# A first Fourier stage issued in half steps: four PSUM banks at once become two and two, three half units apart

## The chip, the cores and the metric

The kernel runs on one core of a Trainium2 chip. The metric is the device time of one execution in microseconds; the kernel before takes 2130.23 us (median of three runs, 2129.25 to 2134.58).

## What is computed

The reference chains three parts. The first transforms `x` (8 batches of 3072 rows and 256 columns, float32) along the rows, mixes its columns, and transforms it back:

```
X = np.fft.rfft(x, axis=1)
Xr, Xi = (X.real.astype(np.float32), X.imag.astype(np.float32))
Yr = Xr @ w_r - Xi @ w_i + b_r
Yi = Xr @ w_i + Xi @ w_r + b_i
Yr = np.sign(Yr) * np.maximum(np.abs(Yr) - lam, 0.0)      # Yi the same
y = np.fft.irfft(Y, n=x.shape[1], axis=1)
```

The second is a two-layer perceptron on all 24576 rows (256 to 2048 to 256, the hidden layer being a squared relu), and the third a soft mixture of 8 experts with 4 slots each. The change is in the first part alone.

## The kernel before

The transform of 3072 points is done as 48 times 64. **Stage A** is the transform of 48 points, **stage B** that of 64, then come the mixing of the columns (**L** and **S**) and the way back (**C**, and D in the next part). Intermediate results go through DRAM: `ad` after stage A, `zd` after stage C. TensorE does all products; VectorE (DVE), ScalarE (ACT) and GpSimd (POOL) take results out of PSUM, split them into a high and a low part and apply the threshold; nearly all transfers of this part are issued on SP's queue, in program order.

A **step** j of stage A (32 of them, four to a batch) takes two tiles `xt` of the input. `a_mm(j, q)` for q = 0 and 1 makes four products of 48 rows by 64 columns, one in each quadrant of the array, into two PSUM banks `psA`; each product is two instructions, so a step is two times eight. `a_out(j, q, r, copy)` copies one bank into half of the tile `sa` of r; with q = 1 the tile is complete, and its two writes to `ad` are issued. There are two buffers of the tag `sa`, so the first copy of a step for r waits until the write of the step before for the same r has landed. `load_x` fetches the tiles of the step after next; there are four `xt` buffers, so it must wait until `a_mm` has used the old ones.

Five steps are done ahead of the loop. The rest, 27, are woven into a loop over **half units** h from 0 to 203 (two to each of 96 units U), whose order is written out by hand and kept on every engine. In an even half TensorE gets `b_mm(U)` (psB), `l_mm(U-2)` (psL and psS) and then `first_stage`; in an odd half `c_mm(U-4)` (psC, only when U is odd) and then, at its end, `first_stage`. The consumers follow one half or one unit later: `b_hi` and `b_sum` on ACT, `b_lo`, `l_move` (L309, L310) and `l_soft` (L320) on DVE, the low part `Sl` on POOL, `c_out` on ACT. All products of this part share one pool of eight PSUM banks (`pbank`, tag `g`): a product waits until the former holder of its bank has been read.

`starts(j)` places the 27 steps at h = 0, 5, 10, 16, 22, 28 and so on, six halves apart. In its half a step is issued whole, followed by its four loads of `xt`; in each of the next four halves ACT copies one bank out. The writes to `ad` therefore come three and four halves after the step.

At the end of each half from h = 17 on, a generator `decode` is advanced, which fetches the perceptron's weights in 32 pieces (`raw`, two buffers) and works on them on all engines. It asks for piece n+1 when it begins with piece n, so the transfer stands in SP's queue behind all that was issued earlier, the step's loads of `xt` included. DVE's first instruction on a piece (L382) waits for its landing and holds up all that DVE has behind it.

Of the kernel before, what the change touches and what calls it, by code (L numbers as in the profile page):

```python
# [103 lines left out]
def fft_moe_kernel(ctx, tc, x, w_r, w_i, b_r, b_i, moe_w_in, moe_w_out, moe2_phi, moe2_w1, moe2_w2,  # L104
                   c_f1, c_bm, c_cm, c_dm, c_st, out):
    nc = tc.nc
    NB = x.shape[0]
# [17 lines left out]
    def drain(it):  # L125
        for _ in it:
            pass
# [26 lines left out]
    def weight_tiles():  # L154
        for q in range(NW):
            wia.append(wpool.tile([128, 4, 2, 128], F32R, tag=f"wia{q}", name=f"wia{q}"))
            wib.append(wpool.tile([128, 3, 2, 128], F32R, tag=f"wib{q}", name=f"wib{q}"))

    def early(tag, name):

        if tag.startswith("wia"):
            t = f(wpool.tile([128, 4, 2, 128], F32R, tag=tag, name=name).rearrange("p a b n -> p (a b n)"))
        else:
            t = wg[:, int(tag[2:])]
        return t.rearrange("p (a d) -> p a d", d=DM)
# [18 lines left out]
    NA = N2 // 16  # L184
# [3 lines left out]
    def pbank(name):  # L188
        return psP.tile([128, 512], F32, tag="g", name=name)

    def load_x(c):
        if c >= XL or c in xt:
            return
        b, k = divmod(c, NC)
        if c < NC:
            t = early(f"wia{c}", f"xt{c}")
        else:
            t = wka.tile([128, TX, DM], F32, tag="xt", name=f"xt{c}", bufs=XB)
        xv = x[b].rearrange("(n1 n2) d -> n1 n2 d", n2=N2)
        m = TX // 2 if c == 0 else TX  # L200
        for o in range(0, TX, m):
            for r in range(2):
                n = 16 * (k // 2) + 8 * r + 4 * (k % 2) + o
                nc.sync.dma_start(t[64 * r:64 * r + N1, o:o + m], xv[:, n:n + m])
        xt[c] = t

    def a_mm(j, q):
        b = j // NA
        if b not in ad:
            ad[b] = dram.tile([N1, N2, DM], F32, tag="ad", name=f"ad{b}", bufs=3)  # L210
        ps = [pbank(f"psA{j}_{q}_{r}").rearrange("p (a d) -> p a d", a=2) for r in range(2)]
        for r in range(2):
            for c in range(2):
                nc.tensor.matmul(ps[r][64 * c:64 * c + 64], lhsT=f1t[64 * r:64 * r + N1],  # L214
                                 rhs=xt[2 * j + c][64 * r:64 * r + N1, 2 * q:2 * q + 2], start=True, stop=True)
        for r in range(2):
            pa[j, q, r] = ps[r]
        if q:
            xt.pop(2 * j)
            xt.pop(2 * j + 1)  # L220

    def a_out(j, q, r, copy):
        i = 2 * j + r
        b, k = divmod(i, 2 * NA)
        if q == 0:
            sa[i] = early(f"wo{k}", f"sa{i}") if b == 0 else wka.tile([128, TX, DM], F32, tag="sa", name=f"sa{i}")
        copy(sa[i][:, 2 * q:2 * q + 2], pa.pop((j, q, r)))
        if q:
            t = sa.pop(i)
            for c in range(2):  # L230
                n = 8 * k + 4 * c
                (nc.sync if b else nc.scalar).dma_start(out=ad[b][:, n:n + TX], in_=t[64 * c:64 * c + N1])

    def load_b(u):
        b, k = divmod(u, NU)
        t = wkb.tile([128, 4, DM], F32, tag="bt", name=f"bt{u}")
        for ch in range(2):
            r = NP * ch + 2 * k
            nc.sync.dma_start(t[N2 * ch:N2 * ch + N2], ad[b][r:r + 4].rearrange("q n d -> n q d"))
        bt[u], bt[u + 1] = t[:, :2], t[:, 2:]  # L240
# [36 lines left out]
    def b_sum(u, eng):  # L277
        sf = sp[u].pop()
        h = wkb.tile([128, 2, 128], F32R, tag="Sh", name=f"Sh{u}")
        l = wkb.tile([128, 2, 128], F32R, tag="Sl", name=f"Sl{u}")  # L280
        split(h, l, sf, eng)
        sp[u] += [h, l]
# [206 lines left out]
    with tc.manual_schedule():  # L489
# [20 lines left out]
        EX = 1 if NB > 1 else 0  # L510
# [10 lines left out]
        def copy(j):  # L521
            return nc.scalar.copy if j % 2 else nc.vector.tensor_copy

        done = []
# [30 lines left out]
        nc.vector.tensor_copy(bias[1], bias[0])  # L555
        nc.vector.tensor_copy(bias[1][0:1, 1], bias[0][0:1, 0])
        dec_run = decode()
        aj = NA + EX
        if NB > 1:
            load_x(12)  # L560
            load_x(13)
# [5 lines left out]
        def at(u, *steps):  # L567
            if 0 <= u < NT:
                for g in steps:
                    g(u)  # L570

        def starts(j):
            j -= NA + EX
            return 5 * j if j < 3 else 16 + 6 * (j - 3)

        for h in range(2 * NT + 12):
            U, o = divmod(h, 2)

            def first_stage():
                nonlocal aj  # L580
                if aj < NB * NA and h == starts(aj):
                    for q in range(2):
                        a_mm(aj, q)
                        done.extend((aj, q, r) for r in range(2))
                    load_x(2 * aj + 4)
                    load_x(2 * aj + 5)
                    aj += 1
                elif done:
                    a_out(*done.pop(0), nc.scalar.copy)

            if o == 0:
                at(U, b_mm)
                at(U - 2, l_mm)
                at(U - 4, l_soft)
                at(U - 1, b_lo)
                at(U - 5, c_out)
                first_stage()
                at(U - 3, l_relu)
            else:
                at(U - 4, c_mm)  # L600
                at(U - 2, l_move)
                at(U, b_hi)
                at(U - 1, lambda u: b_sum(u, nc.gpsimd))
                first_stage()
                if U % 2 and U + 3 < NT:
                    load_b(U + 3)

            if h % 4 == 2 and h < 18:
                nc.sync.dma_start(bm[:, h + 6:h + 10], c_bm[:, h + 6:h + 10])
            if h % 4 == 1 and h < 24:  # L610
                nc.sync.dma_start(cm[:, h // 2:h // 2 + 2], c_cm[:, h // 2:h // 2 + 2])
            if h == 8:
                next(dec_run)
            if h == 14:
                nc.sync.dma_start(ident, c_st[:, 0])
                nc.sync.dma_start(dmt, c_dm)
                nc.sync.dma_start(phi, moe2_phi.rearrange("(a p) n -> p a n", p=128))
                nc.vector.memset(ss, 0.0)
                nc.vector.memset(nm[0], 3.0e38)
            if h == 16:  # L620
                weight_tiles()
            if h > 16:
                for _ in range(1 + (h % 4 == 0)):
                    next(dec_run, None)
            if U == NT - YL and o == 1:
                drain(dec_run)
                wkax.close()
                zp = wgt.enter_context(tc.tile_pool(name="zp", bufs=1, reuse_waits="tile"))
                yp[0] = ypx.enter_context(tc.tile_pool(name="yp0", bufs=1, reuse_waits="tile"))
                ylead = stage_d(0, pbank, nc.vector)  # L630
            if ylead is not None and U > NT - YL + 1:
                next(ylead, None)
# [258 lines left out]
        for n in range(NM + 2):  # L891
            sb, r = divmod(n, NW)
# [331 lines left out]
```

## Time and profile before

| | us |
|---|---|
| median of three runs | 2130.23 |
| profiled execution, device time | 2138.45 |
| its span, first to last instruction | 2136.7 |
| loop of half units within it | about 41.5 to 530 |
| stage A's last product | about 443 |

The profiled execution is 8.2 us longer than the median of the others. A row of the timeline gives start and duration in us, engine, line, operation, output and inputs, and the number of instructions merged; in brackets the idle time of the engine just before, and what ended it. PE is TensorE's product, PEld its weight load, SPq the queue of SP. The ends of products are modelled, so the time that a group of products takes is read from its first start to the start of the next group.

### The profile page before, as it was taken

What the parts mean: (1) busy time and instruction counts of PE and PEld (TensorE: products, weight loads), DVE (VectorE), ACT (ScalarE), POOL (GpSimd) and SP (SyncE); (2) the same over time, 40 slices, a digit from 0 to 9 for tenths busy, and PEclk for the clock granted to TensorE, in tenths of its full rate; (3) what the DMA queues carried; (4) which work ended last, traced back from release to release, by engine and by line L of the source; (5) the groups of instructions that cost most, each with busy time, mean ns of one, the idle gap of its engine ahead of it and who ended that gap; (6) DMA issues with size and microseconds to landing.
All of it is one profiled execution on the core that took longest, in us unless ns stands there. A gap on an engine that the chain in (4) does not pass through costs nothing.

```text
span 2136.7 us, 55389 instructions
## 1 busy us (share of the span) xinstructions
PE 2067.8 (97%) x22288; PEld 1617.6 (76%) x22288; DVE 1530.6 (72%) x2591; ACT 1272.8 (60%) x2910; POOL 1327.5 (62%) x1583
## 2 busy tenths in 40 slices
PE   7999999999799999999999999999999999999994
PEld 3788788888677777777777777777777777777743
DVE  2666776778377777777777777777777777777743
ACT  2577667765466665666665666666566666556632
POOL 0234333421577788887778888778888777888500
PEclk7999999999899999999999999999999999999995
DMA  8999898863211111111111121111111111111589
GB/s 237 250 233 240 221 240 235 246 174 95 46 27 28 29 35 29 33 37 28 28 35 29 29 43 27 28 28 37 29 30 40 27 28 33 32 29 47 172 311 400
DMA packets 113484, 209.75 MB, mean 98 GB/s; under 512 B 14060, under 2 KB 80620, under 8 KB 106956
## 3 DMA queue, kind: packets, MB, share of 16 engines
q1 hardware_dynamic: 112060, 203.04, 35.3%
q8 instruction: 175, 2.87, 0.6%
q10 hardware_dynamic: 1168, 3.18, 0.4%
q14 instruction: 81, 0.66, 0.1%
HBM read 122.38 MB, written 83.79 MB: 96 GB/s over the span
## 4 chain that ended last, share of the span: by engine, by line
PE 88%; DMA 5%; ACT 2%; DVE 1%; POOL 1%; issue 1%; SPq 1%; ACTq 0%; DVEq 0%; POOLq 0%
PE psX L701 20%; PE psA L701 19%; PE ls L754 9%; PE psZ L701 6%; PE pz_a L765 5%; PE psB L247 4%; PE psC L331 4%; PE psY L459 3%; PE pz L765 3%; PE psA L214 3%; PE pz_x L765 2%; PE psL L117 2%; PE psL L118 2%; PE psL L119 2%; DMA out_dram<-ob 2%; PE psS L119 1%
## 5 line engine op out<-in xcount | busy, mean ns | idle before, releaser
L743 POOL TENSOR_TENSOR wg<-wg 128x384 f32<-128x384 f32 x797 | 716.6, 923 | 318.6 <-ACT wg L739 317.3
L747 DVE STREAM_TRANSPOSE gt<-wg 128x768 f32<-128x768 f32 x512 | 491.2, 964 | 135.9 <-POOL wg L743 133.8
L739 ACT ACTIVATE wg<-psX 128x384 f32<-128x384 f32 x512 | 251.7, 492 | 233.7 <-PE psX L701 195.9
L701 PE MATMUL psX<-yh,wia 128*128 128x384 f32 x1024 | 358.2, 350 | 9.8 <-DVE wg L735 6.9
L701 PE MATMUL psA<-yh,wia 128*128 128x384 f32 x1024 | 362.8, 359 | 0.0
L739 ACT ACTIVATE wg<-wg 128x384 f32<-128x384 f32 x512 | 267.3, 522 | 122.2 <-DVE wg L735 122.1
L701 PEld LDWEIGHTS psA<-yh,wia 128*128 128x128 f32 x1024 | 192.6, 188 | 103.4 <-DVE wg L735 57.6
L123 POOL TENSOR_TENSOR Sl<-Sf,Sh 128x256 fp32r<-128x256 f32 x96 | 75.5, 786 | 275.7 <-ACT Sh L122 245.6
L701 PEld LDWEIGHTS psX<-yh,wia 128*128 128x128 f32 x1024 | 192.5, 188 | 47.0 <-DVE acc L770 19.4
L754 PE MATMUL ls<-wg 128*32 128x384 f32 x2048 | 219.6, 499 | 0.3 <-DVE wg L743 0.3
L765 PE MATMUL pz_x<-gt,wg 32*32 32x512 f32 x1584 | 204.2, 598 | 0.0
L765 PE MATMUL pz<-gt,wg 32*32 32x512 f32 x2976 | 199.9, 598 | 0.0
L708 ACT COPY psX<-psA 128x384 f32<-128x384 f32 x256 | 120.0, 469 | 122.1 <-PE psA L701 121.3
L765 PE MATMUL pz_a<-gt,wg 32*32 32x512 f32 x1584 | 191.8, 594 | 0.0
L743 DVE TENSOR_TENSOR wg<-wg 128x384 f32<-128x384 f32 x227 | 182.3, 804 | 7.1 <-ACT wg L739 6.9
L735 DVE TENSOR_TENSOR wg<-psA,wg 128x384 f32<-128x384 f32 x256 | 135.7, 530 | 62.5 <-PE psA L701 62.3
L701 PE MATMUL psA<-yl,wia 128*128 128x384 f32 x512 | 172.6, 337 | 0.0
L701 PE MATMUL psZ<-yh,wib 128*128 128x384 f32 x512 | 172.5, 337 | 0.0
L701 PE MATMUL psX<-yh,wib 128*128 128x384 f32 x512 | 171.8, 336 | 0.0
L701 PE MATMUL psX<-yl,wia 128*128 128x384 f32 x512 | 171.7, 335 | 0.0
L701 PE MATMUL psA<-yh,wib 128*128 128x384 f32 x512 | 171.7, 335 | 0.0
L735 DVE TENSOR_TENSOR wg<-psX,wg 128x384 f32<-128x384 f32 x256 | 136.2, 532 | 41.8 <-ACT wg L722 29.9
(212 smaller groups left out, 4778.3 us busy)
## 6 DMA issues: line engine op xcount, KB each, us to landing
bt<-ad SPq DMA_DIRECT2D x96, 256.0 KB
zd<-sc SPq DMA_DIRECT2D x96, 256.0 KB
zt<-zd SPq DMA_DIRECT2D x64, 384.0 KB
xt<-in_x_dram SPq DMA_DIRECT2D x126, 192.0 KB
ad<-sa SPq DMA_DIRECT2D x112, 192.0 KB
out_dram<-ob SPq DMA_DIRECT2D x21, 1024.0 KB
wg<-ed SPq DMA_DIRECT2D x124, 96.0 KB
w<-in_moe_w_dram SPq DMA_DIRECT2D x5, 1024.0 KB
```

The lines of the kernel that those rows point to most:

```text
L119: nc.tensor.matmul(o, lhsT=al, rhs=bh, start=False, stop=stop)
L123: (eng or nc.vector).tensor_tensor(out=lo, in0=v, in1=f(hi), op=ALU.subtract)
L247: nc.tensor.matmul(p[:, dh, :, l], lhsT=t[:, l, 128 * dh:128 * dh + 128], rhs=bm[:, 2 * (u % NU) + l], start=True, stop=True)
L331: nc.tensor.matmul(ps[l][:, v], lhsT=cm[w, (u - 1 + v) % NU, c], rhs=ub[v][w, c], start=c == 0, stop=c == 1)
L701: nc.tensor.matmul(p, lhsT=w[:, k, l], rhs=r[:, j], start=start and n == 0, stop=n == 2, skip_group_check=True)
L708: nc.scalar.copy(self.x, self.a)
L735: nc.vector.tensor_tensor(out=self.part(k), in0=p, in1=self.z, op=ALU.add)
L739: nc.scalar.activation(out=t, in_=t if p is None else p, func=AF.Relu)
L743: eng.tensor_tensor(out=t, in0=t, in1=t, op=ALU.mult)
L747: nc.vector.transpose(gt[:, 2 * self.q + a + window(self.s)], self.g[a])
L754: nc.tensor.matmul(lgp[o:o + 32], lhsT=pw[:, 2 * self.q + a], rhs=self.part(k), start=self.first, stop=self.last, skip_group_check=True)
L765: nc.tensor.matmul(ps[a][32 * c:32 * c + 32], lhsT=ee[w, c, k], rhs=gt[w, o:o + NT2, 32 * j:32 * j + 32], start=k == 0, stop=k == NB6 - 1, ...
```

## The change

A step is issued in two halves: `a_mm(j, 0)` at `starts(j)` and `a_mm(j, 1)` three half units later, each followed by two copies in the next two halves. The loads of `xt` follow the second half. Where three banks or more are waiting (only while the steps are five halves apart, at h = 6 and h = 11), DVE copies one and ACT another in the same half.

```diff
-        aj = NA + EX
+        aj, aq = NA + EX, 0
...
             def first_stage():
-                nonlocal aj
-                if aj < NB * NA and h == starts(aj):
-                    for q in range(2):
-                        a_mm(aj, q)
-                        done.extend((aj, q, r) for r in range(2))
-                    load_x(2 * aj + 4)
-                    load_x(2 * aj + 5)
-                    aj += 1
+                nonlocal aj, aq
+                if aj < NB * NA and h == starts(aj) + 3 * aq:
+                    a_mm(aj, aq)
+                    done.extend((aj, aq, r) for r in range(2))
+                    if aq:
+                        load_x(2 * aj + 4)
+                        load_x(2 * aj + 5)
+                        aj += 1
+                    aq = 1 - aq
                 elif done:
+                    if len(done) > 2:
+                        a_out(*done.pop(0), nc.vector.tensor_copy)
                     a_out(*done.pop(0), nc.scalar.copy)
```

## Rows read from the trace of the kernel before

**Rows 1.** The page: span, and one line of its transfers (count, size of one)

```profile
span 2136.7 us, 55389 instructions
...
xt<-in_x_dram SPq DMA_DIRECT2D x126, 192.0 KB
```

**Rows 2.** Windows: stretch, its length, busy us of PE, PEld, DVE, ACT, POOL, clock, DMA share, GB/s

```profile
92.00:99.20 7.20, 5.23 (x46) 5.02 (x44) 3.44 (x9) 3.38 (x9) 0.95 (x1) 1.00 1.07 299
99.20:109.40 10.20, 9.49 (x39) 4.98 (x40) 4.75 (x9) 3.11 (x9) 5.48 (x9) 0.50 0.49 141
...
60.00:90.00 30.00, 29.12 (x242) 24.75 (x243) 20.17 (x37) 19.48 (x43) 4.42 (x6) 1.00 1.04 271
110.00:460.00 350.00, 344.42 (x2831) 288.79 (x2830) 249.38 (x499) 246.02 (x566) 141.35 (x188) 1.00 0.87 230
```

**Rows 3.** Timeline of TensorE, 211 to 235 us: groups of products around a step

```profile
211.82 0.28 PE L119 MATMUL psS<-lwh,Sl 128*128 128x256 f32 x1
212.03 1.95 PE L214 MATMUL psA<-xt,f1t 48*64 48x512 f32 x16
212.51 0.15 PEld L214 LDWEIGHTS psA<-xt,f1t 48*64 48x64 f32 x4 [0.28 <-issue]
212.94 0.15 PEld L214 LDWEIGHTS psA<-xt,f1t 48*64 48x64 f32 x4 [0.28 <-issue]
213.91 1.16 PE L247 MATMUL psB<-bm,bt 128*128 128x128 f32 x8
...
229.44 2.00 PE L331 MATMUL psC<-ub,cm 64*128 64x256 f32 x16
231.37 1.16 PE L247 MATMUL psB<-bm,bt 128*128 128x128 f32 x8
...
234.37 0.28 PE L119 MATMUL psS<-lwh,Sl 128*128 128x256 f32 x1
234.48 1.05 PE L247 MATMUL psB<-bm,bt 128*128 128x128 f32 x8
```

**Rows 4.** Timeline of SP's queue, DVE and TensorE, 229 to 242 us (h = 70 on)

```profile
229.58 1.71 SPq L204 DMA_DIRECT2D xt<-in_x_dram  x4
231.70 0.35 SPq L363 DMA_DIRECT2D raw<-in_moe_w_in_dram  x1
...
237.28 0.29 DVE L382 TENSOR_SCALAR ex<-raw 128x256 int32<-128x256 int32 x1 [6.66 <-DMA raw<-in_moe_w_in_dram]
...
237.59 0.70 PE L331 MATMUL psC<-ub,cm 64*128 64x256 f32 x2
238.63 1.13 PE L331 MATMUL psC<-ub,cm 64*128 64x256 f32 x6 [0.34 <-DVE ub L309]
241.66 1.16 PE L247 MATMUL psB<-bm,bt 128*128 128x128 f32 x8
```

**Rows 5.** Timeline of SP's queue and DVE, 279 to 285 us (h = 88 on)

```profile
279.70 0.37 SPq L363 DMA_DIRECT2D raw<-in_moe_w_in_dram  x1
...
284.49 0.29 DVE L382 TENSOR_SCALAR ex<-raw 128x256 int32<-128x256 int32 x1 [5.01 <-DMA raw<-in_moe_w_in_dram]
```

**Rows 6.** Timeline of SP's queue and DVE, 89 to 97 us (h = 17 on)

```profile
89.67 0.43 SPq L363 DMA_DIRECT2D raw<-in_moe_w_in_dram  x1
...
96.95 0.29 DVE L382 TENSOR_SCALAR ex<-raw 128x256 int32<-128x256 int32 x1 [3.65 <-DMA raw<-in_moe_w_in_dram]
```

**Rows 7.** Timeline of SP's queue, ACT and TensorE, 64 to 76 us (h = 8 to 12)

```profile
64.39 0.80 SPq L232 DMA_DIRECT2D ad<-sa  x2
...
70.99 0.59 ACT L227 COPY sa<-psA 128x512 f32<-128x512 f32 x1 [1.93 <-DMA ad<-sa]
...
73.18 0.60 ACT L227 COPY sa<-psA 128x512 f32<-128x512 f32 x1
...
75.57 0.36 PE L117 MATMUL psS<-lwh,Sh 128*128 128x256 f32 x1 [0.88 <-ACT Xi L256]
```

**Rows 8.** Timeline of TensorE, 353 us: the group right behind a step

```profile
352.91 2.59 PE L331 MATMUL psC<-ub,cm 64*128 64x256 f32 x16 [0.69 <-DVE Sf L265]
```

## The prediction

> **What bounds the kernel now.** I read the page first, then windows over the loop, then the timeline of each engine around single steps, and last the waits of DVE and of SP's queue. The change touches only the loop of half units, some 490 of the 2136.7 us of the span [rows 1]; what it wins or loses there shifts all the rest. In that loop TensorE sets the pace: from 110 to 460 us it is busy for 344.4 of 350 us, at the full clock (granted 1.00, 2.4 GHz), while DVE has 249 and ACT 246 [rows 2]. The transfers come next, with a DMA share of 0.87 there and of 1.04 from 60 to 90 us: early in the loop they are saturated [rows 2]. So a microsecond more of products is a microsecond more of time, and what can be won is TensorE's stalls, which are few: 5.6 us by the busy time in that stretch, some more by the starts of groups, since ends are modelled.
>
> I went through those stalls. The largest do not come from banks. DVE stands at L382 and waits for a piece of `raw` that was asked for late, and TensorE runs out of operands behind it. At h = 70 DVE is idle for 6.66 us; SP had issued the four loads of `xt` at 229.58, because they wait for the step's products, and the piece only behind them, at 231.70 [rows 4]. The group psC that then began at 237.59 took 4.07 us to the next start, where such a group takes 1.93 [rows 3, 4]: 2.1 us lost. The same at h = 88 cost DVE 5.01 us [rows 5]. At h = 17 DVE lost 3.65 us [rows 6]; TensorE was then idle for 2.0 of 7.2 us, and its granted clock fell to 0.50 (1.2 GHz) for the next 10.2 us [rows 2], which is 5.1 us of products lost. Of waits on banks I find little: 0.69 us of idle time behind one step [rows 8] and 0.34 us within the group at 238.63 [rows 4].
>
> **The products (term A).** No product is added, but a step becomes two groups. A group of sixteen takes from 212.03 to 213.91, 1.88 us [rows 3]. It runs in waves of four: 0.48 to 212.51, then 0.43 to 212.94, 0.43 again, and 0.54 to the next start (1.88 - 0.48 - 0.43 - 0.43). A group of eight should take the first and the last of these, 1.02 us; two take 2.04, so a step costs 0.16 more. On the way in, psS to psA takes 0.21 us where psS to psB takes 0.11 (211.82 to 212.03 against 234.37 to 234.48 [rows 3]), 0.10 more. Counted from the loop, 14 of the 27 second halves stand behind psS and 13 elsewhere, mostly behind psC, where I add nothing, since psC pays for leaving its own form already. 27 x 0.16 + 14 x 0.10 = **+5.7 us**, all on the path, since TensorE is the bound. No row shows a group of eight in the loop; if leaving the form cost nothing it would be +1.4, if each entry cost 0.10 it would be +7.
>
> The rows thus show a price of about a quarter microsecond for entering and leaving the group of small products. The Trainium skill (TensorEngine Tiling (Array Packing), Key Properties) says that changing the tiling mode drains TensorE, which speaks against cutting a group in two. By that rule the 13 entries that I left free, from psC's form into psA's, would drain too and pay 0.10 us each, and A would be +7.0 instead of +5.7, the sum 1.3 us higher; no row here shows that entry.
>
> **The queue of SP (terms B to D).** The four loads of `xt` move from phase 0 of a step to phase 3, with their wait for TensorE; the writes of `ad` move from phases 3 and 4 to 4 and 5. Behind each stand the loads `bt`, the writes `zd` and the pieces `raw`. From the generator I counted in which phase each piece is asked for. *B:* two pieces with only two half units to land are asked for in phase 0, at h = 70 and 88. They are freed: -2.1 us, and -1.5 for the other (5.01 us of idle time against 6.66; ends 0.5 and 2.1). Together **-3.6 us** (0 to -4.2). *C:* at h = 17 the four loads of 192 KB [rows 1] of the step at h = 16 no longer stand ahead in a saturated queue; 768 KB at 271 GB/s [rows 2] are 2.8 us of the 3.65. I take the stall and the slow clock as gone: -2.0 - 5.1 = **-7.1 us** (0 to -9). *D:* the pieces at h = 97 and 115 now stand behind the loads in phase 3. An idle time of 6.66 us cost 2.1, so one that grows by 2 to 3 us costs about 0.8: **+1.5 us** for both (0 to +4). `bt` itself is issued about 1 us later in half the steps; it is asked for five half units ahead and TensorE waits for it nowhere in the loop, so nothing.
>
> **The buffers `sa` (terms E and F).** This is the new wait. A write now starts one half unit later, while the next step's copies keep their places. While steps are five halves apart it is worse: at h = 6 and h = 11 the last bank of the old step and the first of the new one are copied in the same half, and one half later ACT wants the buffer whose write has only just been issued. How long a write takes to land there: issued at 64.39, it released ACT at 70.99, 6.6 us later, and ACT had stood for 1.93 us [rows 7]; TensorE then missed 0.88 us at psS, through ACT's `Xi` and `Sh`, which are queued behind the copy [rows 7]. Now the write of h = 11 will be issued at about 72 and land at about 78, while the copy that wants the buffer stood at 73.18 [rows 7]: ACT is held for 5 us instead of 2. Behind it are `sc`, `ua`, `Xh`, `Xi`, `Sh`, and POOL's `Sl` and TensorE's psS and psL wait for these. Taking off the 1 us that a hold may last without harm (1.93 against 0.88), TensorE loses 4 us. At h = 7 the same on a smaller scale, 1 us. A stall of 4 us may lower the clock, as at 99.20 [rows 2]; I take 3 us for that, more than half of the 5.1. *E* is **+8 us** (+2 to +11). *F:* with steps six halves apart three halves remain instead of four, 1.5 units of 490 / 102 = 4.8 us or 7 us, against 4.8 to 6.6 us from issue to landing [rows 4, 5, 7]. No such wait stands in the profile after 100 us; I put **+1 us** (0 to +3).
>
> **The banks (term G).** The banks psA are held for 1, 2, 1 and 2 halves instead of 1, 2, 3 and 4, and eight are shared by all. That removes the waits of rows 8 and the 0.34 us of rows 4, and spreads a step's time over the units: **-1.5 us** (0 to -4). ACT has two copies less, DVE two more; nothing.
>
> **The sum.** 5.7 - 3.6 - 7.1 + 1.5 + 8 + 1 - 1.5 = +4.0 us. On the profiled execution (device time 2138.45 us, 1.75 around the span) this gives 2142.5; it is 8.2 us above the median, perhaps because of its slow stretch at 99 us, which the others need not have had. On the median it is **2134 us**. A measurement here can tell about 0.3%, 6.4 us, from no change.
>
> **Rivals.** *The new hold decides* (slower): ACT stands at h = 7 and h = 12 until the writes land, TensorE stalls for 5 us and the clock falls, and the slow stretch at h = 17 was not in the median's runs, so C brings nothing. 5.7 - 3.6 + 1.5 + 10 + 1 - 1.5 = +13, 2143 us. For it: the landing of 6.6 us and the saturated DMA; against it: DVE takes one copy over, and a delay there lets the transfers catch up. It decides from a hold of about 2 us on. *The stalls go and the cut is cheap* (faster): B, C and G come in full, E is the 2 us of its lower end. 5.7 - 4.2 - 7.1 + 1 + 2 - 4 = -6.6, 2123.6 us. For it: rows 4 to 6 name a cause that the change does move; against it: the same loads then stand ahead of other pieces. *It changes nothing* because TensorE's stalls only move: 2130 us.
>
> **How the numbers follow.** The forecast (2129 to 2138 us) gets 0.45, the slower rival 0.27, the faster one 0.20, no change at all 0.08. The forecast lies on both sides of the bound of 6.4 us, mostly within it. So faster by over 0.3% (under 2123.8): 0.17; within: 0.48; slower (over 2136.6): 0.35. The range must reach into both rivals: 2122 to 2145 us.
>
> **What would show it.** In the profile after: groups psA of eight, 1.02 us to the next start (A); the pieces at h = 70 and 88 issued right behind the piece before, DVE's waits for `raw` there gone (B); the clock between 92 and 116 us at 1.00 (C); larger waits at h = 97 and 115 (D); ACT at L227 waiting for `ad` at about 62 and 73 us for 3 and 5 us, with a stall of TensorE behind it (E). The forecast is wrong if groups of eight cost well under 1 us or over 1.2, if ACT waits for `ad` in most of the 27 steps, or if TensorE is starved by `bt` or `xt`.

## The result and the profile after

The kernel after takes 2142.59 us (median of four runs, 2141.44 to 2144.11), the kernel before 2131.81 us on the same chip. The ratio is 1.0051, with a 95% interval of 1.0033 to 1.0068: the change costs 10.9 us (7.0 to 14.5), which is more than the 0.3% that can be told from no change. The profiled executions stand closer together, 2141.44 us after against 2138.45 before; the one of before holds the slow stretch at 99 us [rows 2].

First the same windows as in [rows 2]; the span is 2138.9 us. The columns are the stretch, its length, busy time of PE, PEld, DVE, ACT and POOL, the granted clock, the DMA share and GB/s.

```profile
92.00:99.20 7.20, 7.20 (x62) 6.17 (x62) 6.16 (x12) 4.79 (x12) 3.74 (x5) 1.00 1.03 209
99.20:109.40 10.20, 10.20 (x84) 8.36 (x82) 6.68 (x17) 7.50 (x17) 6.52 (x10) 1.00 1.06 323
60.00:90.00 30.00, 28.72 (x227) 22.45 (x230) 21.15 (x39) 18.94 (x43) 4.74 (x7) 1.00 0.92 255
110.00:460.00 350.00, 339.26 (x2735) 277.05 (x2735) 240.31 (x481) 237.15 (x547) 135.87 (x182) 1.00 0.81 224
```

The slow stretch at 99 us is gone. But from 110 to 460 us TensorE is now idle for 10.7 us where it was idle for 5.6 [rows 2], and the DMA share fell from 0.87 to 0.81. In that window the extra cost of cutting a group counts as busy time, so the 5.1 us more are stalls alone.

Next what ended the idle time of DVE and ACT between 46 and 460 us: who waited, for what, us in total, times, longest.

```profile
DVE ex L382 <- DMA raw<-in_moe_w_out_dram: 18.3, 5, 6.5
...
DVE ex L382 <- DMA raw<-in_moe_w_in_dram: 9.5, 4, 4.4
...
ACT sa L227 <- DMA ad<-sa: 48.2, 15, 5.4
```

The same view of before, which has only one wait for `ad`:

```profile
DVE ex L382 <- DMA raw<-in_moe_w_in_dram: 15.3, 3, 6.7
...
DVE ex L382 <- DMA raw<-in_moe_w_out_dram: 7.7, 4, 2.3
...
ACT sa L227 <- DMA ad<-sa: 1.9, 1, 1.9
```

DVE waits for `raw` 27.8 us in nine places instead of 23.0 in seven, and not at the same pieces: the waits at h = 17, 70 and 88 [rows 4 to 6] have shrunk to these (DVE's timeline after, start, duration, instruction, idle time before it):

```profile
91.89 0.29 DVE L382 TENSOR_SCALAR ex<-raw 128x256 int32<-128x256 int32 x1 [1.07 <-POOL v L395]
...
227.99 0.30 DVE L382 TENSOR_SCALAR ex<-raw 128x256 int32<-128x256 int32 x1 [1.89 <-POOL v L395]
...
275.86 0.29 DVE L382 TENSOR_SCALAR ex<-raw 128x256 int32<-128x256 int32 x1 [0.62 <-DMA raw<-in_moe_w_in_dram]
```

Other pieces wait instead, though not both that term D named: the one asked for at h = 97 waits for 0.29 us only. The largest wait is that of the piece asked for at h = 115 (2.13 us of idle time before the change). Timeline after of SP's queue, DVE and TensorE there:

```profile
341.11 1.72 SPq L204 DMA_DIRECT2D xt<-in_x_dram  x4
342.88 1.26 SPq L239 DMA_DIRECT2D bt<-ad  x2
344.24 0.55 SPq L363 DMA_DIRECT2D raw<-in_moe_w_out_dram  x1
...
351.54 0.29 DVE L382 TENSOR_SCALAR ex<-raw 128x256 int32<-128x256 int32 x1 [6.48 <-DMA raw<-in_moe_w_out_dram]
...
348.22 1.13 PE L331 MATMUL psC<-ub,cm 64*128 64x256 f32 x8
352.90 1.39 PE L331 MATMUL psC<-ub,cm 64*128 64x256 f32 x8 [3.55 <-DVE ub L320]
354.22 2.07 PE L247 MATMUL psB<-bm,bt 128*128 128x128 f32 x8
```

The four loads of `xt`, now in phase 3, stand right ahead of the piece. SP had issued nothing since 334 us, because these loads wait until the second half of the products has used their buffers; then all that stood behind them was issued in one run. The DMA share of 0.81 is a mean of such empty and full stretches (second number from the end):

```profile
338.00:342.00 4.00, 4.00 (x34) 2.70 (x34) 3.26 (x8) 2.41 (x6) 1.20 (x2) 1.00 0.00 0
342.00:354.00 12.00, 8.45 (x70) 6.65 (x68) 4.26 (x10) 3.94 (x11) 2.17 (x3) 0.99 1.03 266
```

The piece was issued at 344.24 and used at 351.54; DVE stood for 6.48 us, and the group psC took 6.00 us to the next start instead of 1.93. Behind that stall the clock was granted at 0.51 for 3.4 us (third number from the end):

```profile
348.20:353.60 5.40, 1.85 (x18) 1.35 (x16) 2.06 (x6) 0.66 (x2) 0.00 (x0) 1.00 1.05 337
353.60:357.00 3.40, 3.40 (x18) 2.81 (x16) 3.27 (x7) 3.40 (x11) 1.28 (x2) 0.51 0.74 176
```

Pieces asked for in phases 4 and 5 suffer likewise: at h = 27, 44, 80, 105 and 140 DVE's idle time grew from 1.29, 1.07, 2.27, 1.07 and 0.63 us to 3.10, 3.72, 4.75, 3.47 and 4.36.

The same four loads also stand ahead of the writes `ad`. Timeline after of SP's queue, TensorE and ACT around the step at h = 40:

```profile
151.34 2.24 SPq L204 DMA_DIRECT2D xt<-in_x_dram  x4
153.63 1.26 SPq L239 DMA_DIRECT2D bt<-ad  x2
154.99 1.25 SPq L345 DMA_DIRECT2D zd<-sc  x2
156.33 1.86 SPq L232 DMA_DIRECT2D ad<-sa  x2
...
157.42 1.09 PE L214 MATMUL psA<-xt,f1t 48*64 48x512 f32 x8
158.44 2.00 PE L331 MATMUL psC<-ub,cm 64*128 64x256 f32 x16
...
162.02 0.59 ACT L227 COPY sa<-psA 128x512 f32<-128x512 f32 x1 [4.00 <-DMA ad<-sa]
```

The two writes of the step before were issued from 156.33 on, at the end of that run; the later one had landed at 161.92, and only then could ACT take out the bank that was filled by 158.44. Over the stretch from 110 to 460 us, the median write takes 4.7 us from issue to landing, where it took 3.7 before. Both kinds of wait often end together: ACT goes on at 162.02, 256.20 and 418.93, DVE with the pieces asked for at h = 44, 80 and 140 at 162.60, 256.77 and 419.83.

### The profile page after: what moved, and what is told of

Read it like the earlier page. It is cut to its first block, busy times and chain, and to the rows that moved or that the text cites. A ratio compares the mean times of both kernels' runs of the same rounds, so it can differ in the third digit from the quotient of the medians.

```text
span 2138.9 us, 55408 instructions
## 1 busy us (share of the span) xinstructions
PE 2065.6 (97%) x22288; PEld 1609.9 (75%) x22288; DVE 1533.0 (72%) x2593; ACT 1271.2 (59%) x2908; POOL 1324.9 (62%) x1583
## 4 chain that ended last, share of the span: by engine, by line
PE 86%; DMA 5%; ACT 3%; issue 2%; POOL 2%; DVE 1%; SPq 1%; ACTq 0%; DVEq 0%; POOLq 0%
PE psX L704 20%; PE psA L704 19%; PE ls L757 9%; PE psZ L704 6%; PE pz_a L768 5%; PE psC L331 4%; PE psB L247 4%; PE psY L459 3%; PE pz L768 3%; PE psA L214 2%; PE pz_x L768 2%; PE psL L117 2%; PE psL L118 2%; PE psL L119 2%; DMA out_dram<-ob 2%
## 5 line engine op out<-in xcount | busy, mean ns | idle before, releaser
L704 PEld LDWEIGHTS psX<-yh,wia 128*128 128x128 f32 x1024 | 192.4, 188 | 47.1 <-DVE acc L773 19.4
L704 PE MATMUL psA<-yh,wib 128*128 128x384 f32 x512 | 171.2, 334 | 0.0
```

The costliest lines, as they stand in the source:

```text
L704: nc.tensor.matmul(p, lhsT=w[:, k, l], rhs=r[:, j], start=start and n == 0, stop=n == 2, skip_group_check=True)
```

## The experiments

Each kernel was timed beside the kernel before on the same chip; differences in us are the ratio's, at 2131.8 us. The last column is TensorE's idle time in the window from 110 to 460 us of the profiled execution.

| kernel | ratio (95%) | us against before | idle 110 to 460 |
|---|---|---|---|
| before | 1 | 0 | 5.6 |
| after | 1.0051 (1.0033 to 1.0068) | +10.9 | 10.7 |
| before, only the cut | 1.0011 (0.9998 to 1.0024) | +2.3 | 2.9 |
| before, only later copies | 1.0021 (1.0008 to 1.0034) | +4.5 | 6.0 |
| before, only later loads | 1.0059 (1.0044 to 1.0074) | +12.6 | 13.6 |
| before, later loads, three `raw` | 0.9977 (0.9965 to 0.9989) | -4.9 | 3.0 |
| before, three `raw` | 0.9969 (0.9958 to 0.9979) | -6.6 | 2.9 |
| before, three `raw`, six `sa` | 0.9978 (0.9966 to 0.9990) | -4.7 | 2.9 |
| after, six `sa` | 1.0039 (1.0025 to 1.0053) | +8.3 | 8.6 |
| after, three `raw` | 1.0017 (1.0002 to 1.0031) | +3.6 | 4.7 |
| after, three `raw`, six `sa` | 0.9970 (0.9957 to 0.9983) | -6.4 | 0.9 |
| after, loads early again | 1.0012 (1.0001 to 1.0023) | +2.6 | 0.8 |
| after, loads early, six `sa` | 0.9996 (0.9982 to 1.0011) | -0.9 | 2.2 |
| after, halves two apart | 1.0010 (0.9997 to 1.0024) | +2.1 | 5.1 |

**One part of the change at a time.** The first kernel cuts the group of sixteen products in two; the first eight go between psB and psL of the same half unit, and nothing else moves.

```diff
-                    for q in range(2):
+                    for q in range(o == 0, 2):
                         a_mm(aj, q)
...
+                if aj < NB * NA and h == starts(aj):
+                    a_mm(aj, 0)
```

> The kernel before with only the products cut: where a step stands in an even half unit (26 of the 27 steps), its first eight products go between psB and psL and the other eight stay behind psS. Loads, copies and writes stay where they were. Theory 'the cut itself costs': two groups of eight at 1.02 us instead of one of 1.88, and one more entry, 0.16 to 0.26 us a step, so 4 to 7 us slower than before. Rival 'the cut is free, all the loss is in the waits': within 1 us of before.

Measured 2133.87 us, +2.3 (-0.4 to +5.1). In the two traces the starts of psB at units 12 and 78 lie 3.9 us further apart than before. The time lies between theory and rival and is not clear of zero; by the starts the cut does cost. Either way it is not the loss.

The second keeps the step whole and moves its last two copies, and so the writes, one half later:

```diff
-                elif done:
+                elif done and (h < 16 or h != starts(aj - 1) + 3):
```

> The kernel before with products and loads as they were; only the last two copies of each step, and with them the writes of ad, come one half unit later, from h = 16 on (the 24 steps that are six apart). Theory 'the write of one step holds the copies of the next': ACT waits at L227 for ad in about ten steps, some 20 to 40 us in all, and the time grows by 2 to 5 us. Rival 'ACT has room for it': the waits appear, but the time stays within 1 us of before.

Measured 2135.06 us, +4.5 (1.7 to 7.2). Its profile does not show where: ACT waits for `ad` three times, 3.9 us in all, not the ten times and 20 to 40 us of the theory, and from unit 12 on the loop runs as before (336.1 us to unit 78, before 336.0). Where the timed runs lose it stays open.

The third leaves products and copies as they were and issues only the loads of `xt` three halves later:

```diff
-                    load_x(2 * aj + 4)
-                    load_x(2 * aj + 5)
...
+            def late_loads():
+                j = aj - 1
+                if j >= NA + EX and h == starts(j) + 3:
+                    load_x(2 * j + 4)
+                    load_x(2 * j + 5)
...
                 first_stage()
+                late_loads()
```

> The kernel before with products and copies as they were; only the four loads of xt of each step come three half units later. Theory 'the loads hold up whatever stands behind them': DVE's waits for raw at h = 70 and 88 go (6.7 and 5.0 us to under 2), that at h = 115 grows from 2 to 5 us or more; the sum is within 3 us of before, so this part does not explain a loss of 11 us. Rival 'the queue explains it': 6 us slower or more.

Measured 2142.99 us, +12.6 (9.4 to 15.8), as the rival said: this move alone costs as much as the whole change. DVE's waits in its profile, 46 to 460 us:

```profile
DVE ex L382 <- DMA raw<-in_moe_w_out_dram: 23.7, 6, 5.8
DVE ex L382 <- DMA raw<-in_moe_w_in_dram: 13.6, 5, 4.4
```

And its window:

```profile
110.00:460.00 350.00, 336.39 (x2707) 280.39 (x2708) 238.33 (x479) 235.40 (x542) 135.35 (x181) 0.98 0.81 224
```

DVE stands for `raw` 37.3 us in eleven places, TensorE is idle for 13.6 us, and the clock fell four times behind the stalls (at 62.0, 171.2 and 263.4 us for 3.4 us each and at 355.5 for 6.8). Here the loads do not wait for products: SP's waits for psA at L204, 62.9 us from 110 to 460 us in after and 58.1 in before, are gone. So the loads cost as much from a late place in the queue without that wait.

The three parts by themselves add up to 19.4 us, the change costs 10.9. The second kernel also keeps two banks psA one half longer, which the change does not; how much of the difference that is, is not shown.

**Does it go through the pieces?** The following edit gives the pieces three buffers and asks for each one piece earlier, so that they have about nine half units to land.

```diff
-tag="raw", name=f"raw{n}", bufs=2)
+tag="raw", name=f"raw{n}", bufs=3)
...
         load(0)
+        load(1)
...
-            load(n + 1)
+            load(n + 2)
```

It was made in three kernels: in the one with late loads only, in before, and in after.

> The kernel before with the loads of xt three halves later (which alone gave +12.7 us) and with three buffers raw. It tells whether the late loads cost through the pieces raw or in another way. Theory (through raw): nearly all of the +12.7 goes, so within 3 us of the kernel before with three buffers raw, about 2127. Rival (xt arrives late, or writes zd and ad behind the loads hold up ACT): most of it stays, 2138 or more, and ACT's wait for zd at L341 (17.7 us in the run with late loads alone) stays too.

> The kernel before with three buffers raw, each piece asked for one piece earlier. It prices the stalls of term B and C in the kernel before, by taking away their cause. Theory: the waits at h = 17, 70 and 88 vanish (15 us of DVE's idle time), TensorE gains the 3.6 us of term B and 0 to 2 of term C, so 2124 to 2127 us against 2130.3. Rival: TensorE does not gain what DVE loses, since the units' work catches up behind: 2129 to 2131.

> The kernel after with three buffers raw instead of two, each piece asked for one piece earlier, so that a piece has about nine half units to land instead of four. Theory: most of the loss of the change goes through DVE standing at L382 for pieces that now queue behind the later loads of xt. Then DVE's waits for raw of 2 to 6.5 us vanish, TensorE's stalls between unit 12 and unit 75 shrink by 6 to 8 us, and the time falls from 2142.6 to about 2135; what stays above the kernel before is the cut (+3) and the holds (+3). Rival: the loss is made by the writes and loads of the loop bunching in the queue (bt, zd and ad land late, ACT stands for them), whatever DVE waits for: then the time stays within 2 us of 2142.6 and the stalls stay, with ACT or TensorE waiting for transfers instead.

With late loads 2130.07 us, -4.9 (-7.5 to -2.3); before 2127.24 us, -6.6 (-9.0 to -4.5). So late loads cost 12.6 us with two buffers and 1.7 with three: nearly all of their cost in the kernel before goes through the pieces, as the first theory said. And the kernel before had lost 6.6 us to late pieces all along, 3 us more than the 3.6 of the stalls at h = 70 and 88.

After: 2136.37 us, +3.6 (0.4 to 6.6). It gains 7.2 us, as expected, but so does the kernel before: beside that one the change still costs 10.2. DVE no longer waits for `raw` at all; ACT does wait for `ad`, as much as before this edit. ACT's line L227 in that kernel, 110 to 460 us (what ended the idle time before it, us, times):

```profile
  DMA ad<-sa: 29.2, 11
```

**The holds on `sa`.** Six buffers in memory of the second weight that is free at that time, so that no copy into `sa` waits for a write (the profile calls these buffers `wg`):

```diff
-early(f"wo{k}", f"sa{i}") if b == 0 else wka.tile([128, TX, DM], F32, tag="sa", name=f"sa{i}")
+early(f"wo{k if b == 0 else i % 6}", f"sa{i}")
```

In after, alone and with three buffers `raw`, and in before with three buffers `raw`:

> The changed kernel with six buffers sa in the loop instead of two (they lie in a tile that the loop does not use), so that a copy never waits for the write of the step before. Theory 'the holds cost half of the loss': ACT's 48 us of waits for ad go, and the kernel falls from 10.8 us above before to 4 to 7 us above it. Rival 'only the cut and the queue count': it stays at 9 us or more above before.

> The kernel after with both: six buffers sa and three buffers raw. What is left of the change is the cut in two groups (+2.4 to 3.6 measured alone, +5.7 by the starts) and the freer banks (term G, 0 to -4). Theory: if the pieces cost 6 to 8 and the holds 3.2 and both are independent, 2132 to 2133. Rival, the holds and the pieces cover each other (DVE's delay lets the writes land): the gains do not add, 2134 to 2136.

> The kernel before with three buffers raw and six buffers sa: the same two aids that took the kernel after from 2142.6 to 2126.4. The difference between the two is what the change itself is worth once neither the pieces nor the writes hold anybody up: the cut (term A, +2.4 to 5.7) against the freer banks (term G, 0 to -4). The kernel before has few holds on sa, so six of them give at most 1 us over three buffers raw alone (2127.2). Theory: 2125.5 to 2127, so A and G cancel to within 2 us. Rival, the holds of the kernel before cost as much as those of after: 2121 to 2123, and the change is worth +4 by its products alone.

Alone 2139.39 us, +8.3 (5.3 to 11.3), between theory and rival: the holds give only 2.6 us back. On top of three buffers `raw` they give 10: 2126.41 us, -6.4 (-9.2 to -3.6), where 2132 at best had been expected. The gains do not add, they help each other. With six `sa` alone DVE still waits 29.8 us for `raw`, with three `raw` alone ACT still waits 45.3 us for `ad`; the loop stalls in either, for 8.6 and 4.7 us of its window. With both, TensorE is idle for less than 1 us in 350:

```profile
110.00:460.00 350.00, 349.08 (x2863) 288.99 (x2866) 251.99 (x497) 244.84 (x562) 139.00 (x185) 1.00 0.83 230
```

The kernel before with the same two aids takes 2126.56 us, -4.7 (-7.2 to -2.1), with 2.9 us idle in its window:

```profile
110.00:460.00 350.00, 347.14 (x2855) 291.16 (x2852) 254.81 (x500) 245.18 (x564) 137.97 (x185) 1.00 0.85 230
```

So once nobody waits for a piece or for a write to `ad`, the change is worth nothing that can be measured (-1.7 us, within the intervals); in the traces the way from unit 12 to unit 78 takes 332.9 us with it and 333.3 without. ACT still waits for writes to `zd` in both (L341, 18.7 us with the change, 5.2 without), and TensorE does not stand for it. What pays for the cut is fewer stalls: in that window the kernel before with both aids still has three over 0.5 us by the starts of groups, the kernel after with both has none. Two of them (0.80 and 0.59 us) are at the group psC right behind a step, where its weight loads wait for DVE (L309, which reads psL), presumably for a bank; the largest (1.22 us) is ahead of a step, where psS waits for POOL's `Sl` and not for a bank. That the banks alone pay is therefore not shown.

**The loads alone put back.** The kernel after with six buffers `xt`, so that the loads can go in phase 0 without a wait (the two buffers `sa` moved into the free memory of the second weight to make room):

```diff
-    XB, XL = 4, NB * NC
+    XB, XL = 6, NB * NC
...
-                    if aq:
+                    if aq == 0:
                         load_x(2 * aj + 4)
                         load_x(2 * aj + 5)
-                        aj += 1
+                    aj += aq
```

and the same with six buffers `sa`.

> The kernel after with six buffers xt, its loads of xt back in phase 0, behind the first half of the products, where no buffer is waited for (the two buffers sa lie in free memory of the second weight, nothing else is moved). It undoes the move of term D alone, with two buffers raw. Theory (the late loads in SP's queue are the main loss): the time falls by 6 to 9 us to 2134 to 2137, about as with three buffers raw (2136.4), and DVE's waits for raw at h = 44, 80, 105, 115 and 140 fall below 2.5 us. Rival (the writes ad in phases 4 and 5 hold the pieces up as much): 2139 or more, the waits at h = 44, 80 and 140 stay at 3 us and more.

> The kernel after with six buffers xt, loads in phase 0, and six buffers sa. Six buffers sa alone gave 3.2 us, and 10 us on top of three buffers raw. Theory: the holds on sa and the late pieces cover each other, so that taking away one leaves part of the other's loss; then this is 2126 to 2130. Rival, the gains simply add: 2131 to 2133.

The first takes 2132.71 us, +2.6 (0.2 to 4.9): 8.3 us of the 10.9 go with the place of the loads and with their wait for the products, within the 6 to 9 of its theory. DVE's waits at h = 44, 80, 105, 115 and 140 are down to 0.67, 0.83, 1.07, 1.10 and 1.62 us, as its theory said; those at h = 70 and 88 come back to 3.3 and 3.4 us, behind the loads in phase 0. What was not expected: ACT's waits at L227 vanish too, though writes and copies are where the change put them. The idle time before L227 from 110 to 460 us, in after:

```profile
  DMA ad<-sa: 32.7, 10
```

the same in this kernel:

```profile
  DMA ad<-wg: 0.9, 1
```

and this kernel's window:

```profile
110.00:460.00 350.00, 349.18 (x2861) 288.79 (x2860) 254.48 (x505) 247.79 (x566) 140.51 (x187) 1.00 0.89 231
```

The median write lands 3.4 us after its issue here, against 4.7. So the holds of the steady loop went with the loads that stood right ahead of the writes. Before 110 us ACT still waits 14.3 us in four places (15.5 in five after), while the steps are five halves apart; the change itself makes these. Behind the last of them, 5.36 us long, TensorE is busy for 1.66 of the 4.0 us up to 82.4, and then its clock is at 0.51 for 3.5 us.

With six buffers `sa` as well it takes 2130.96 us, -0.9 (-3.8 to +2.3), at the lower end of the rival's range: here the gains add within the intervals, since the one aid had taken most of both waits. It stays 5.5 us above the kernel after with three buffers `raw` and six `sa`, in line with the 6.6 us that these gave before: the pieces at h = 17, 70 and 88 still cost DVE 3.9, 2.9 and 4.8 us.

**Two half units apart instead of three.** One number of the change; the loads then come in phase 2, and DVE copies one bank of each step, so the writes come in phases 3 and 4 as before.

```diff
-                if aj < NB * NA and h == starts(aj) + 3 * aq:
+                if aj < NB * NA and h == starts(aj) + 2 * aq:
```

> The kernel after with the second half of a step two half units behind the first instead of three. The loads of xt come in phase 2, and since three banks are then waiting, DVE copies one of them and the writes ad come in phases 3 and 4, as before the change. The cut is the same. Theory: the holds on sa are those of before, the pieces asked for in phases 3 to 5 have one half, 2.4 us, more behind the loads: 2134 to 2138. Rival (any late load costs what three halves cost): 2140 or more.

2134.09 us, +2.1 (-0.6 to +5.1). ACT waits for `ad` 7.4 us instead of 48.2, DVE for `raw` 27.6 us still, in ten places, but for 4.8 us at most instead of 6.5; the longest idle time of TensorE from 110 to 460 us is 1.6 us, where it was 3.55. One half unit is worth 8.8 us, most of the loss. That it is because ACT and DVE no longer wait at the same time is likely, but this run does not show it: the loads, the copies and the writes all moved.

## Why the prediction was right or wrong

The time lies in the range, 8.6 us above the likeliest case, and beyond the bound of 0.3%, which had been given 0.35 against 0.48 for no change. That the range held is partly luck: it was 23 us wide, and errors of both signs met in it. The time is near the 2143 us of the slower rival, yet that rival's mechanism, the new hold at h = 7 and 12 with its fall of the clock, is not what carries the loss. Term by term:

**A, the cut: right by the starts.** A group of eight takes 1.02 us and the way in 0.09 us more than psB does. TensorE after:

```profile
210.38 2.00 PE L331 MATMUL psC<-ub,cm 64*128 64x256 f32 x16
212.31 1.09 PE L214 MATMUL psA<-xt,f1t 48*64 48x512 f32 x8
213.33 1.16 PE L247 MATMUL psB<-bm,bt 128*128 128x128 f32 x8
...
227.78 0.28 PE L119 MATMUL psS<-lwh,Sl 128*128 128x256 f32 x1
227.99 1.09 PE L214 MATMUL psA<-xt,f1t 48*64 48x512 f32 x8
229.01 1.16 PE L247 MATMUL psB<-bm,bt 128*128 128x128 f32 x8
```

213.33 - 212.31 and 229.01 - 227.99 are both 1.02. The group psC ahead of a step takes 212.31 - 210.38 = 1.93 us, as it does ahead of psB [rows 3], so the entry from there adds nothing, as assumed. That makes 5.7 us. The kernel with the cut alone measured 2.3 (-0.4 to +5.1), but it cuts at another place and TensorE idles for 2.7 us less in its window, so the two figures need not be equal. The Trainium skill's rule (TensorEngine Tiling (Array Packing), Key Properties) that a change of tiling mode drains TensorE fits the 0.09 us at the entry from psS. The 1.3 us that the prediction worked out by it for the entries from psC did not come; this does not contradict the rule, because psC's products (64*128) also change form on the way to psB (128*128), and both ways take 1.93 us.

**B, the freed pieces: right** by the trace. At h = 70 and 88 DVE's idle time went from 6.66 and 5.01 us to 1.89 and 0.62, and the group psC that had taken 4.07 us takes 1.92 (232.18 to 234.10). No run measures this gain by itself.

**C, the piece at h = 17 and the slow clock: the stall went, the gain did not reach the median.** In the profiled execution it is real: psB of unit 12 starts at 100.0 us instead of 109.2. But the text said that the median's runs need not have had the slow stretch, and then took its 7.1 us off the median all the same. The 24 runs of before that were timed with the first experiments lean the same way: the ten that took 2133 us and more have a mean clock of 0.975 to 0.979, the fourteen below 2131 one of 0.978 to 0.981. That fits a stretch which some runs have and some don't, though where the clock fell in them is not shown. Three buffers `raw` in before take away the waits of B and C together, and more, and gave 6.6 us (4.5 to 9.0), where the two terms make 10.7.

**D, the loads ahead of other pieces: the step that failed.** It was priced at 1.5 us (0 to 4), for the two pieces asked for in phase 3. Late loads alone measured 12.6, and putting them back in the changed kernel gave 8.3. Of the two pieces one waited (6.48 us at h = 115), the other hardly (0.29 us at h = 97). Three things were missing. The pieces of phases 4 and 5 stand behind the loads as well, since the run of transfers has not ended by then (a DMA share of 1.03 until 354 us). The price per piece was taken from one case, 2.1 us lost for 6.66 us of idle time; at h = 115 in the changed kernel TensorE lost 4.1 us for 6.48, and 1.7 more by the clock. And the writes `ad` stand behind the loads too, which is F.

**E, the hold while steps are five apart: the waits right, their price too high.** ACT stood at L227 for 5.42 and 4.45 us, where 3 and 5 had been forecast. ACT and TensorE after, up to 78 us:

```profile
58.92 0.59 ACT L227 COPY sa<-psA 128x512 f32<-128x512 f32 x1 [5.42 <-DMA ad<-sa]
...
71.83 0.59 ACT L227 COPY sa<-psA 128x512 f32<-128x512 f32 x1 [4.45 <-DMA ad<-sa]
...
61.23 0.39 PE L117 MATMUL psS<-lwh,Sh 128*128 128x256 f32 x1 [0.43 <-ACT Sh L122]
...
77.06 0.39 PE L117 MATMUL psS<-lwh,Sh 128*128 128x256 f32 x1 [0.24 <-ACT Sh L122]
```

TensorE lost 1.3 us behind the first (59 to 63 us) and 0.7 at the end of the groups behind the second (77 us), and the clock stayed at 1.00 through both. Six buffers `sa` bring psB of unit 9 forward by 2.5 us against unit 0 in the traces, by 3.6 where there are three `raw` as well. So E is about 2.5 to 3.6 us, not 8. The rule that a hold costs all but its first microsecond was wrong. The 3 us for the clock did not come here, but the idea was not empty: in the kernel with six `xt` such a hold was followed by 3.5 us at half clock.

**F, the hold later on: wrong.** "No such wait stands in the profile after 100 us" was true of before, where writes do not follow loads. After has ten, 32.7 us. With the pieces out of the way six `sa` win 7.4 us in the traces from unit 12 on, not the 1 us forecast (0 to 3); with the pieces still late it is 2.6. With the loads put back the waits of the steady loop are down to 0.9 us: F failed at the same step as D.

**G, the banks: right in sign, size open.** The kernel after with both aids is as fast as before with both, although the cut is in it: something gives back about what A takes, between the 2.3 us measured for the cut and the 5.7 of its starts, where 1.5 was forecast and 4 was the bound. The intervals of the two kernels, nearly 3 us either way each, do not exclude 1.5, and the largest of the three stalls that went was not at a bank.

Sum by measurement: 2.3 for the cut, 8.3 for the place of the loads and 2.6 for the remaining holds make 13.2; 10.9 came, so 2.3 us are left as the gain of G. B and C are within the 8.3, since the loads put back bring waits at h = 70 and 88 back. Against the forecast of 4.0 us on the median, D was too low by 7, B and C together too high as a gain by 4 or more, and E too dear by 4 to 5.5: two errors of one sign and one of the other. With about 3 us of interval on each figure this explains the 8.6 us only roughly.

## What to carry to other kernels

When a step moves, follow each of its transfers to its new place in the queue, and list everything asked for behind it until the queue is empty, not just the next entry: pieces, writes, and the buffers that the writes hold. Two waits that end at about the same time hide each other, so taking away one of them shows less than its price; test them together as well as alone. A buffer more for data that is fetched far ahead (here 2 KB a partition for `raw`) took the place in the queue out of the matter, and was itself worth 6.6 us in the kernel before.

## What the runs showed of the hardware

A mean share of the transfers hid how they came. In the changed kernel the DMA share from 110 to 460 us was 0.81, but it was 0.00 from 338 to 342 us and 1.03 from 342 to 354. Writes behind four loads of 192 KB took a median of 4.7 us from issue to landing there, against 3.4 in the kernel with a mean share of 0.89 where the loads were not right ahead of them. These runs do not part the order of issue from the crowding in such a run of transfers.

The granted clock fell to half (1.2 GHz) behind stalls of TensorE of quite different kinds. After one of 3.55 us (348.2 to 353.6 us in the changed kernel) it was 0.51 for 3.4 us. After two of 0.70 and 0.85 us close together it was 0.50 for 3.4 us too; this is the kernel with late loads alone:

```profile
168.00:171.20 3.20, 1.65 (x12) 1.24 (x11) 3.08 (x7) 3.20 (x9) 2.47 (x3) 1.00 0.44 130
171.20:174.60 3.40, 3.40 (x17) 2.73 (x18) 3.23 (x11) 1.52 (x4) 0.95 (x2) 0.50 0.93 255
```

Yet 2.7 us of idle time from 255 to 262 us in the changed kernel left it at 1.00:

```profile
255.00:262.00 7.00, 4.31 (x33) 2.93 (x32) 5.03 (x10) 5.02 (x12) 1.29 (x2) 1.00 0.78 228
```

So the length of a stall alone does not tell whether the clock falls behind it.
